# One addition of epsilon and one reciprocal for two blocks of attention probabilities

## The chip, the cores and the metric

The kernel runs on one core of a Trainium2 chip. The time is device microseconds (us) of one execution, and the number compared is the median of the runs.

## What is computed

Three stages follow each other: block-causal attention (4 batches, 8 heads, 576 positions, 64 per head, blocks of 64), a squared-ReLU feed-forward layer on 2304 tokens, and a top-1 mixture of 8 experts. The change touches the first stage alone. Cut to it, the reference is:

```python
scores = q @ k.T / sqrt(64)
scores = where(block_i >= block_j, scores, -1e9)
scores = scores - max(scores)
attn = exp(scores)
attn = attn / (sum(attn) + 1e-9)
out = attn @ v
```

## The kernel before, in words

Attention works on *units*: two heads of one batch, 16 units in all. A unit has nine *blocks* of 64 query rows; with both heads a block fills 128 partitions, and block i sees (i + 1) * 64 keys. So there are 144 steps, one block each, and the loop at L230 runs the parts of several blocks in each step, by three lags (`LAGS = (1, 5, 7)`, L279):

- `scores` (L129) of the block of this step: on GpSimd a memset of 64 columns where i is even (L135); on TensorE three fp32r matmuls (L146), or one fp32 matmul for blocks 0 and 1 (L143); on VectorE the negated row maximum from PSUM (L148); on ScalarE the exponential with the maximum as bias, which also writes the row sum into the small tile `sm` (L153). Block 8 is done in two halves of 288 columns, whose maxima are joined at L151 and whose two sums stand in the two columns of `sm`.
- `normalise` (L157) of the block of one step ago: on VectorE `sm + 1e-9` into `rc` (L164; for block 8, with two sums, L162) and its reciprocal (L165); on GpSimd the product of the block's probabilities `p` with `rc` (L166), 64 to 576 columns wide.
- `p_transpose` (L168) of the block of five steps ago: transpositions of the scaled probabilities on TensorE (L185) and copies from PSUM to SBUF on ScalarE (L191). Blocks 0 and 1, and 2 and 3, are transposed together, when the second of them is due; blocks 4 to 8 each in a step of its own.
- `pv` (L195) seven steps behind blocks 3 and 8: the products with V on TensorE (L208).

In between come, for the next unit, the transpositions of Q and K (L93) and their split in a high and a low part (ScalarE L102 to L126, VectorE L86 and L88, called at the end of the step by `flush`). Weights of the feed-forward layer are converted beside the attention (`convert`, one chunk every four steps from step 8 to step 80, L582): three integer operations on VectorE (L336 to L338), one cast on ScalarE (L371) and one subtraction on GpSimd (L342). From step 50 on, pieces of the feed-forward layer (L385, L460) are run beside the attention.

The tiles of `p` have six buffers, the scores four PSUM banks in the first 36 steps and three after, the transpositions three banks, then two. No order is written out by hand in this stage: the framework's planner fills each engine's queue, starting from the order of the program, the dependencies, the free buffers and its own estimates of durations. On the chip each queue is then worked off strictly in that order.

Of the kernel before, what the change touches and what calls it, by code (L numbers as in the profile page):

```python
# [9 lines left out]
F32 = mybir.dt.float32  # L10
# [4 lines left out]
ALU = mybir.AluOpType  # L15
AX = mybir.AxisListType
PSUM = bass.MemoryType.PSUM
P = 128


def attention(nc, tc, ctx, ps, ident, q, k, v, xT_d):
# [7 lines left out]
    B, H, S, D = q.shape  # L29
# [9 lines left out]
    small = pool("a_small", 8)  # L39
# [16 lines left out]
    st = {}  # L56
# [25 lines left out]
    def flush():  # L82
        while todo:
            scale, o, src, high = todo.pop(0)
            if scale:
                nc.vector.scalar_tensor_tensor(o, src, 0.125, high.bitcast(F32), ALU.mult, ALU.subtract)  # L86
            else:
                nc.vector.tensor_sub(o, src, high.bitcast(F32))  # L88
# [19 lines left out]
    def q_transpose(u):  # L108
        q_high(u, transpose4(st[u]["raw"][0]), slice(0, 8))

    def k_transpose(u):
        kh = kt.tile([P, S], F32R, name="kh", tag="kh")
        kl = kt.tile([P, S], F32R, name="kl", tag="kl")
        kf = kt.tile([P, P], F32, name="kf", tag="kf")
        st[u]["k"] = (kh, kl, kf)
        t = transpose4(st[u]["raw"][1])
        nc.scalar.copy(kf, t[:, 0:P])
        nc.scalar.copy(kh[:, 0:512], t)
        low(False, kl[:, 0:512], t, kh[:, 0:512])

    def tails(u):
        t = ps.t.tile([P, 512], F32, name="te", tag="t")
        nc.tensor.transpose(t[:, 0:P], st[u]["tail"].rearrange("p h d -> p (h d)"), ident)
        q_high(u, t[:, 0:D], slice(8, 9))
        kh, kl, _ = st[u]["k"]
        nc.scalar.copy(kh[:, 512:], t[:, D:2 * D])  # L126
        low(False, kl[:, 512:], t[:, D:2 * D], kh[:, 512:])

    def scores(u, i):  # L129
        kh, kl, kf = st[u]["k"]  # L130
        qh, ql = qb[u % 2]
        n = (i + 1) * D
        pr = pp.tile([P, 640], F32, name="p", tag="p")
        if i % 2 == 0:
            nc.gpsimd.memset(pr[:, n:n + D], 0.0)  # L135
        parts = [(0, n)] if i < 8 else [(0, 288), (288, 288)]
        nm = small.tile([P, 2], F32, name="nm", tag="nm")
        sm = small.tile([P, 2], F32, name="sm", tag="sm")
        scs = []
        for e, (k0, w) in enumerate(parts):  # L140
            sc = ps.s.tile([P, 512], F32, name="sc", tag="s")
            if i < 2:
                nc.tensor.matmul(sc[:, 0:w], qf[u % 2][:, i].rearrange("p h d -> p (h d)"), kf[:, 0:w],  # L143
                                 start=True, stop=True)
            for j, (a, kk) in enumerate(((qh, kh), (qh, kl), (ql, kh)) if i >= 2 else ()):
                nc.tensor.matmul(sc[:, 0:max(w, 256)], a[:, i - 2].rearrange("p h d -> p (h d)"),  # L146
                                 kk[:, k0:k0 + max(w, 256)], start=(j == 0), stop=(j == 2))
            ps.last["max"] = nc.vector.tensor_reduce(nm[:, e:e + 1], sc[:, 0:w], AX.X, ALU.max, negate=True)  # L148
            scs.append(sc)
        if len(parts) == 2:  # L150
            nc.vector.tensor_tensor(nm[:, 0:1], nm[:, 0:1], nm[:, 1:2], ALU.min)  # L151
        for e, (k0, w) in enumerate(parts):
            ps.last["exp"] = nc.scalar.activation(pr[:, k0:k0 + w], scs[e][:, 0:w], AF.Exp, bias=nm[:, 0:1],  # L153
                                                  accum_out=sm[:, e:e + 1])
        st[u][i] = (pr, sm, len(parts))

    def normalise(u, i):  # L157
        n = (i + 1) * D
        pr, sm, k_ = st[u][i]
        rc = small.tile([P, 1], F32, name="rc", tag="rc")  # L160
        if k_ == 2:
            nc.vector.tensor_scalar(rc, sm[:, 0:1], sm[:, 1:2], 1e-9, ALU.add, ALU.add)  # L162
        else:
            nc.vector.tensor_scalar_add(rc, sm[:, 0:1], 1e-9)  # L164
        nc.vector.reciprocal(rc, rc)  # L165
        ps.last["scale"] = nc.gpsimd.tensor_mul(pr[:, 0:n], pr[:, 0:n], rc.to_broadcast([P, n]))  # L166

    def p_transpose(u, blocks):  # L168
        i0 = blocks[0]
        grp = int(i0 >= 4)  # L170
        if i0 == 4 * grp:
            st[u]["pt", grp] = pt.tile(([P, 4, 2, P], [P, 5, 5, P])[grp], F32, name=f"pt{grp}", tag=f"pt{grp}")
        out = st[u]["pt", grp]
        nch = i0 // 2 + 1
        jobs = []
        if grp == 0:
            jobs.append(([(i, c) for i in blocks for c in range(nch)], out[:, i0:i0 + 2, 0:nch]))
        else:
            for c0, c1 in ((0, min(4, nch)), (4, nch)):
                if c1 > c0:  # L180
                    jobs.append(([(i0, c) for c in range(c0, c1)], out[:, i0 - 4, c0:c1]))
        for lst, o in jobs:
            t = ps.t.tile([P, 512], F32, name="tp", tag="t")
            for e, (i, c) in enumerate(lst):
                nc.tensor.transpose(t[:, e * P:(e + 1) * P], st[u][i][0][:, c * P:(c + 1) * P], ident)  # L185
            src = t[:, 0:len(lst) * P]
            if grp == 0:
                src = src.rearrange("p (i c n) -> p i c n", i=2, n=P)
            else:
                src = src.rearrange("p (c n) -> p c n", n=P)  # L190
            P_COPY(nc, i0)(o, src)  # L191
        for i in blocks:
            st[u].pop(i)
# [32 lines left out]
    def at(t):  # L226
        return seq[t] if 0 <= t < len(seq) else (None, None)

    done = 0
    for t in range(len(seq) + LP + 1):  # L230
        u, i = at(t - LT)
        if i in (1, 3):
            p_transpose(u, [i - 1, i])
        elif u is not None and i >= 4:
            p_transpose(u, [i])
        u, i = at(t)
        if u is not None:
            scores(u, i)
            if u + 1 < NU:
                with tc.issue_after(ps.last["exp"].ins) if u == 0 else nullcontext():  # L240
                    if i == 4:
                        q_transpose(u + 1)
                    if i == 5:
                        k_transpose(u + 1)
                if i == 6:
                    tails(u + 1)
            if i == 1 and u == 0:
                load(1, QK)
            if i == (8 if u else 3):
                load(u + 1, V)  # L250
            if i == 7:
                load(u + 2, QK)
        u, i = at(t - LN)
        if u is not None:
            normalise(u, i)
        flush()
        u, i = at(t - LP)
        if i == 3:
            pv(u, 0)
        if i == 8:  # L260
            pv(u, 1)
            done += 1
        yield done
# [1124 lines left out]
```

## Time and profile before

| | |
|---|---|
| median of 3 runs | 909.71 us (908.70 to 909.87) |
| profiled execution, its time | 910.21 us |
| its span, first to last instruction | 908.5 us |
| TensorE busy (share of the span) | 879.4 us (97%) |
| VectorE busy | 640.2 us (70%) |
| ScalarE busy | 569.8 us (63%) |
| GpSimd busy | 217.7 us (24%) |
| granted TensorE clock, mean | 0.996 |

All durations below are from the profiled execution. PE is TensorE's matmul side and PEld its loading of weights, DVE is VectorE, ACT ScalarE, POOL GpSimd. A row of the timeline reads: start, duration (of the whole row, where it merges several instructions), engine, line, operation, output <- input, shape, count; in brackets the idle time of the engine ahead of it and what ended it. Matmuls overlap, so a TensorE that is busy all the time can still have some room.

### The profile page before, as it was taken

What the parts mean: (1) busy time and instruction counts of PE and PEld (TensorE: products, weight loads), DVE (VectorE), ACT (ScalarE), POOL (GpSimd) and SP (SyncE); (2) the same over time, 40 slices, a digit from 0 to 9 for tenths busy, and PEclk for the clock granted to TensorE, in tenths of its full rate; (3) what the DMA queues carried; (4) which work ended last, traced back from release to release, by engine and by line L of the source; (5) the groups of instructions that cost most, each with busy time, mean ns of one, the idle gap of its engine ahead of it and who ended that gap; (6) DMA issues with size and microseconds to landing.
All of it is one profiled execution on the core that took longest, in us unless ns stands there. A gap on an engine that the chain in (4) does not pass through costs nothing. (4 is left out here: it accounts for less than half of the span.)

```text
span 908.5 us, 17049 instructions
## 1 busy us (share of the span) xinstructions
PE 879.4 (97%) x5765; PEld 726.4 (80%) x5765; DVE 640.2 (70%) x1490; ACT 569.8 (63%) x1165; POOL 217.7 (24%) x335
## 2 busy tenths in 40 slices
PE   6889999999999999999999999999999999999996
PEld 5666777888878789999999999998477776776775
DVE  5889986464645446878967777766688888676783
ACT  6888785575757544333566665542287777776773
POOL 4676674142333200000000000002024322222110
PEclk9999999999999999999999999999999999999998
DMA  5766543322220133445112222115345696636601
GB/s 146 174 177 185 143 115 78 100 53 76 77 73 28 54 113 101 155 140 178 56 47 67 74 62 60 44 47 194 109 163 215 229 380 251 223 131 247 197 13 39
DMA packets 109481, 113.84 MB, mean 125 GB/s; under 512 B 62679, under 2 KB 80617, under 8 KB 109387
## 3 DMA queue, kind: packets, MB, share of 16 engines
q1 hardware_dynamic: 105579, 100.74, 35.6%
q0 software_dynamic: 3808, 11.94, 3.7%
q8 instruction: 48, 0.79, 0.4%
q14 instruction: 46, 0.38, 0.2%
HBM read 143.58 MB, written 19.80 MB: 180 GB/s over the span
## 5 line engine op out<-in xcount | busy, mean ns | idle before, releaser
L385 PE MATMUL ph<-xh,wih 128*128 128x256 f32 x576 | 165.8, 288 | 0.0
L385 PE MATMUL ph<-xh,wil 128*128 128x256 f32 x576 | 162.2, 282 | 0.0
L385 PE MATMUL ph<-xl,wih 128*128 128x256 f32 x576 | 162.0, 281 | 0.0
L166 POOL TENSOR_TENSOR p<-p,rc 128x64 f32<-128x64 f32 (+2 forms) x144 | 111.6, 784 | 119.5 <-DVE rc L165 56.7
L385 PEld LDWEIGHTS ph<-xh,wih 128*128 128x128 f32 x576 | 109.0, 189 | 5.3 <-issue 3.1
L385 PEld LDWEIGHTS ph<-xl,wih 128*128 128x128 f32 x576 | 109.2, 190 | 1.1
L385 PEld LDWEIGHTS ph<-xh,wil 128*128 128x128 f32 x576 | 109.2, 190 | 0.4 <-issue 0.4
L148 DVE TENSOR_REDUCE nm<-sc 128x1 f32<-128x288 f32 (+8 forms) x160 | 70.3, 449 | 54.1 <-PE sc L146 45.9
L153 ACT ACTIVATE p<-sc,nm 128x288 f32<-128x288 f32 (+8 forms) x160 | 80.6, 507 | 18.6 <-DVE nm L148 8.1
L1012 DVE TENSOR_TENSOR w1l<-raw,w1h 128x1024 fp32r<-128x1024 f32 x60 | 71.7, 1222 | 23.0 <-ACT w1h L1011 20.5
L1012 DVE TENSOR_TENSOR w2l<-raw,w2h 128x1024 fp32r<-128x1024 f32 x64 | 75.4, 1219 | 10.8 <-ACT w2h L1011 10.7
L1020 POOL DMA_INDIRECT xr<-x_d,gidx_e x2 | 2.3, 1130 | 310.4 <-PE ph L385 310.1
L185 PE MATMUL tp<-ident,p 128*128 128x128 f32 x400 | 65.3, 278 | 6.8 <-POOL p L166 4.5
L395 ACT ACTIVATE r<-ph 128x512 f32<-128x512 f32 x44 | 26.3, 597 | 72.0 <-PE ph L385 71.8
L1011 ACT CAST w2h<-raw 128x1024 fp32r<-128x1024 f32 x64 | 66.1, 1050 | 7.7 <-PE py L1115 7.5
L1011 ACT CAST w1h<-raw 128x1024 fp32r<-128x1024 f32 x60 | 61.6, 1050 | 9.4 <-PE ph L1098 8.7
L191 ACT COPY pt<-tp 128x512 f32<-128x512 f32 (+3 forms) x128 | 61.7, 499 | 8.7 <-PE tp L185 8.2
L185 PEld LDWEIGHTS tp<-ident,p 128*128 128x128 f32 x400 | 46.1, 142 | 18.7 <-POOL p L166 9.5
L396 DVE SCALAR_TENSOR_TENSOR r<-r,sc 128x512 f32<-128x512 f32 x44 | 34.7, 788 | 36.5 <-ACT r L395 36.2
L208 PE MATMUL o<-pt,raw_v 128*64 128x320 f32 (+4 forms) x448 | 55.9, 366 | 1.1 <-ACT pt L191 1.1
L1115 PE MATMUL py<-w2h,hh 128*128 128x512 f32 x128 | 52.1, 407 | 0.0
L1115 PE MATMUL py<-w2h,hl 128*128 128x512 f32 x128 | 50.8, 397 | 0.0
(306 smaller groups left out, 2269.2 us busy)
## 6 DMA issues: line engine op xcount, KB each, us to landing
raw<-in_moe_w_dram SPq DMA_DIRECT2D x172, 512.0 KB
xr<-xT_d SPq DMA_DIRECT2D x19, 512.0 KB
wr<-in_moe_w_in_dram SPq DMA_DIRECT2D x16, 512.0 KB
wr<-in_moe_w_out_dram SPq DMA_DIRECT2D x16, 512.0 KB
row<-part_d SPq DMA_DIRECT2D x20, 256.0 KB
x_d<-row SPq DMA_DIRECT2D x18, 256.5 KB
xT_d<-x SPq DMA_DIRECT2D x16, 288.0 KB
raw_q<-in_q_dram SPq DMA_DIRECT2D x32, 128.0 KB
```

Of the source, the lines that this page charges most:

```text
L148: ps.last["max"] = nc.vector.tensor_reduce(nm[:, e:e + 1], sc[:, 0:w], AX.X, ALU.max, negate=True)
L153: ps.last["exp"] = nc.scalar.activation(pr[:, k0:k0 + w], scs[e][:, 0:w], AF.Exp, bias=nm[:, 0:1], accum_out=sm[:, e:e + 1])
L166: ps.last["scale"] = nc.gpsimd.tensor_mul(pr[:, 0:n], pr[:, 0:n], rc.to_broadcast([P, n]))
L185: nc.tensor.transpose(t[:, e * P:(e + 1) * P], st[u][i][0][:, c * P:(c + 1) * P], ident)
L191: P_COPY(nc, i0)(o, src)
L208: nc.tensor.matmul(o[r, first * D:n], vt[:, c, hh], p[:, first:, c, r], start=(c == 0), stop=(c == cs[-1]))
L385: nc.tensor.matmul(ph[:, e], self.wi[p][w][:, c, e * P:(e + 1) * P], x[a][:, c], start=(n == 0), stop=(n == 3 * KC - 1))
L395: nc.scalar.activation(r, ph.rearrange("p e (t n) -> p (e t) n", n=P), AF.Relu)
L396: nc.vector.scalar_tensor_tensor(r, r, self.sc[:, 0:1], r, ALU.mult, ALU.mult)
L1011: self.nc.scalar.copy(ws[0][c], r)
L1012: self.nc.vector.tensor_sub(ws[1][c], r, ws[0][c].bitcast(F32))
L1115: nc.tensor.matmul(py, hT[a][:, c], self.w2s[w][c // 2][:, c % 2 * D:c % 2 * D + D], start=(t == 0), stop=(t == 3 * KF - 1))
```

## The change

`normalise` is no longer called for every block but for the pairs (0, 1), (2, 3), (4, 5), (6, 7), at the step at which the odd block was normalised before, and for block 8 alone. The two blocks of a pair share one `sm` tile of two columns. One addition and one reciprocal over two columns (128x2 in place of 128x1) give both factors, and GpSimd then does the two multiplications, even block first. The exponentials and the multiplications stay what they were.

```diff
         nm = small.tile([P, 2], F32, name="nm", tag="nm")
-        sm = small.tile([P, 2], F32, name="sm", tag="sm")
+        if i % 2 == 0:
+            st[u]["sm"] = small.tile([P, 2], F32, name="sm", tag="sm")
+        sm = st[u]["sm"]
...
-                                                  accum_out=sm[:, e:e + 1])
-        st[u][i] = (pr, sm, len(parts))
-
-    def normalise(u, i):
-        n = (i + 1) * D
-        pr, sm, k_ = st[u][i]
-        rc = small.tile([P, 1], F32, name="rc", tag="rc")
-        if k_ == 2:
-            nc.vector.tensor_scalar(rc, sm[:, 0:1], sm[:, 1:2], 1e-9, ALU.add, ALU.add)
+                                                  accum_out=sm[:, e + i % 2:e + i % 2 + 1])
+        st[u][i] = (pr, sm)
+
+    def normalise(u, blocks):
+
+        sm = st[u][blocks[0]][1]
+        rc = small.tile([P, 2], F32, name="rc", tag="rc")
+        if len(blocks) == 1:
+            nc.vector.tensor_scalar(rc[:, 0:1], sm[:, 0:1], sm[:, 1:2], 1e-9, ALU.add, ALU.add)
+            nc.vector.reciprocal(rc[:, 0:1], rc[:, 0:1])
         else:
-            nc.vector.tensor_scalar_add(rc, sm[:, 0:1], 1e-9)
-        nc.vector.reciprocal(rc, rc)
-        ps.last["scale"] = nc.gpsimd.tensor_mul(pr[:, 0:n], pr[:, 0:n], rc.to_broadcast([P, n]))
+            nc.vector.tensor_scalar_add(rc, sm, 1e-9)
+            nc.vector.reciprocal(rc, rc)
+        for e, i in enumerate(blocks):
+            n, pr = (i + 1) * D, st[u][i][0]
+            ps.last["scale"] = nc.gpsimd.tensor_mul(pr[:, 0:n], pr[:, 0:n], rc[:, e:e + 1].to_broadcast([P, n]))
...
-        if u is not None:
-            normalise(u, i)
+        if u is not None and (i % 2 or i == 8):
+            normalise(u, [i] if i == 8 else [i - 1, i])
```

## Rows read from the trace of the kernel before

**Rows 1.** Busy time of each engine by stretch; columns as in the first line.

```profile
core 0: us, PE busy (x) PEld busy (x) DVE busy (x) ACT busy (x) POOL busy (x), PEclk, DMA share, GB/s
12.60:82.00 69.40, 59.44 (x422) 45.38 (x421) 60.47 (x203) 61.09 (x201) 47.34 (x81) 1.00 0.65 173
82.00:134.40 52.40, 50.47 (x359) 40.62 (x360) 46.36 (x136) 44.12 (x135) 34.62 (x52) 1.00 0.53 146
134.40:320.00 185.60, 184.25 (x1270) 153.74 (x1269) 97.89 (x308) 117.92 (x340) 65.04 (x131) 1.00 0.24 67
```

**Rows 2.** Groups by line, 12.6 to 82.0 us: busy us, mean ns | idle before.

```profile
L185 PE MATMUL tp<-ident,p 128*128 128x128 f32 x121 | 20.4, 281 | 5.7 <-POOL p L166 4.5 <-ACT pt L191 0.7 <-POOL wil L342 0.3
...
L165 DVE RECIPROCAL rc<-rc 128x1 f32<-128x1 f32 x45 | 6.5, 153 | 0.3
```

**Rows 3.** Lines L164, L151, L336, 12.6 to 82.0 us: ns min/median/max.

```profile
L164 DVE TENSOR_SCALAR rc<-sm x40: 126/142/155, 13.9 to 81.0; 128x1 f32<-128x1 f32 x40
...
L151 DVE TENSOR_TENSOR nm<-nm x5: 146/524/728, 19.8 to 77.4; 128x1 f32<-128x1 f32 x5
...
L336 DVE TENSOR_SCALAR f<-wr x10: 401/712/1262, 23.2 to 81.0; 128x512 int32<-128x512 int32 x10
```

**Rows 4.** Line L779 (the router's addition of epsilon), whole run: ns min/median/max.

```profile
L779 DVE TENSOR_SCALAR sm<-sm x9: 161/167/170, 473.0 to 642.3; 128x2 f32<-128x2 f32 x9
```

**Rows 5.** Timeline around the end of unit 1 (start us, us).

```profile
33.60 0.66 PE L185 MATMUL tp<-ident,p 128*128 128x128 f32 x4
...
34.30 0.59 ACT L191 COPY pt<-tp 128x512 f32<-128x512 f32 x1
34.78 0.51 ACT L153 ACTIVATE p<-sc,nm 128x288 f32<-128x288 f32 x1
34.90 1.04 POOL L166 TENSOR_TENSOR p<-p,rc 128x512 f32<-128x512 f32 x1 [2.68 <-ACT pt L191]
...
37.63 0.33 PE L146 MATMUL sc<-kh,ql 128*128 128x384 f32 x1
38.80 0.77 PE L185 MATMUL tp<-ident,p 128*128 128x128 f32 x5 [0.84 <-POOL p L166]
```

**Rows 6.** Timeline around the end of unit 2.

```profile
47.50 0.94 POOL L166 TENSOR_TENSOR p<-p,rc 128x448 f32<-128x448 f32 x1
...
48.49 0.33 PE L185 MATMUL tp<-ident,p 128*128 128x128 f32 x1 [0.86 <-POOL p L166]
...
48.86 1.04 POOL L166 TENSOR_TENSOR p<-p,rc 128x512 f32<-128x512 f32 x1 [0.42 <-PE tp L185]
...
53.20 0.77 PE L185 MATMUL tp<-ident,p 128*128 128x128 f32 x5 [1.27 <-POOL p L166]
```

**Rows 7.** Timeline around the end of unit 4.

```profile
77.50 0.66 PE L185 MATMUL tp<-ident,p 128*128 128x128 f32 x4
77.78 1.34 POOL L166 TENSOR_TENSOR p<-p,rc 128x512 f32<-128x512 f32 x1 [0.57 <-DVE rc L165]
...
81.99 0.66 PE L185 MATMUL tp<-ident,p 128*128 128x128 f32 x4 [0.68 <-POOL p L166]
```

**Rows 8.** Timeline around the end of unit 0.

```profile
15.90 0.72 POOL L166 TENSOR_TENSOR p<-p,rc 128x320 f32<-128x320 f32 x1
...
18.33 0.50 PE L185 MATMUL tp<-ident,p 128*128 128x128 f32 x3
...
18.80 1.72 POOL L166 TENSOR_TENSOR p<-p,rc 128x384 f32<-128x384 f32 x2 [0.33 <-DVE rc L165]
...
23.79 0.44 PE L185 MATMUL tp<-ident,p 128*128 128x128 f32 x2 [0.49 <-POOL p L166]
```

**Rows 9.** Timeline around the end of unit 3.

```profile
60.41 0.83 POOL L166 TENSOR_TENSOR p<-p,rc 128x384 f32<-128x384 f32 x1 [0.65 <-DVE rc L164]
60.51 0.49 PE L185 MATMUL tp<-ident,p 128*128 128x128 f32 x3
...
62.53 1.08 POOL L166 TENSOR_TENSOR p<-p,rc 128x512 f32<-128x512 f32 x1 [0.23 <-DVE rc L165]
...
64.16 0.60 PE L185 MATMUL tp<-ident,p 128*128 128x128 f32 x4
```

## The prediction

> **What bounds the kernel now.** I read the busy time by stretch first [rows 1], since the page's averages mix stages, and cut it at unit boundaries. From 134.4 us to the end of the attention TensorE is busy for 184.25 of 185.60 us, because pieces of the feed-forward layer fill it; what VectorE or GpSimd do there has cover. The change can only tell ahead of that. From 12.6 to 82.0 us (units 0 to 4, before these pieces) no engine is full: TensorE is busy 59.44 us of 69.40, VectorE 60.47, ScalarE 61.09, GpSimd 47.34. That is a ring of waits between four nearly equally loaded engines, with 9.96 us of TensorE idle; from 82.0 to 134.4 us (units 5 to 7) it is 1.93 us. Then I read what ends TensorE's idle time in the first stretch: 4.5 us of the 5.7 us ahead of the transpositions end with GpSimd's scaling [rows 2]. So the scaled probabilities already come too late for TensorE there, five steps after the scores. Last I read the timeline at the end of each of these five units, where the light blocks 0 to 2 of the next unit make the five steps short [rows 5 to 9]. A reader should look for two starts: that of a scaling on GpSimd and that of the transposition that needs it.
>
> **What goes.** Each of the 64 pairs loses one addition and one reciprocal. In the first stretch that is 20 pairs at 0.142 [rows 3] plus 0.153 us [rows 2], 5.9 us of VectorE. The two that remain have two elements. The nearest row for these is the router's addition of epsilon, the same operation and shape: 0.167 us [rows 4], against 0.142 for one element, so 0.025 more; the reciprocal has no such row, and I give it nothing. That leaves 5.9 - 20 x 0.025 = 5.4 us. How much of it is on the path is bounded by 0 and 5.4. I take a third, 1.8 us: three engines are loaded alike here, and a microsecond of VectorE counts only where its queue is what the others wait for. In units 5 to 7 I take 0 (TensorE's whole idle time of 1.93 us is the bound), and after them 0, covered by the matmuls.
>
> **What is moved.** The scaling of the even block now waits for the odd block's exponential. On the queue of GpSimd the memset of a next `p` tile (L135) and the subtraction of a weight chunk (L342) stand behind this wait; both already stood behind the odd block's own. On VectorE the merged addition waits for what the odd block's addition waited for. No DMA is issued in the moved step, and SyncE's queue isn't passed. For blocks 0 to 3 the wait costs nothing, since a pair is transposed together. Blocks 4 and 6 are transposed alone, one step ahead of their partner. For them I read each unit with one rule: the new scaling of the even block begins where the old one of the odd block began.
>
> - Unit 1: the scaling of block 7 began at 34.90; block 6 takes 0.94 us [rows 6], so it ends at 35.84 where its transposition began at 33.60 [rows 5]: 2.2 us late.
> - Unit 2: 48.86 + 0.94 = 49.80 against 48.49 [rows 6]: 1.3 us.
> - Unit 4: 77.78 + 0.94 = 78.72 against 77.50 [rows 7]: 1.2 us.
> - Unit 0: here it is block 4. Its 0.72 us begin at 18.80 instead of 15.90, and end at 19.52 against a transposition at 18.33: 1.2 us [rows 8]. Block 6 then finds TensorE late already, and I don't count it again.
> - Unit 3: block 4 ends at 60.41 + 0.72 = 61.13 against 60.51, 0.6 us; block 6 would end at 63.47, ahead of 64.16 [rows 9], and costs nothing.
>
> The sum is 6.5 us. Block 7 follows 0.94 us later than now behind block 6, less than block 6's own lateness in units 1, 2 and 4, so it isn't counted a second time. Part of the 6.5 us is absorbed: TensorE waits today for block 8's scaling at the end of the units, 0.49 us in unit 0 [rows 8], 1.27 in unit 2 [rows 6], 0.68 in unit 4 [rows 7], together 2.4 us, and a TensorE that comes late waits that much less. In unit 1 the 0.84 us [rows 5] don't help: on ScalarE the copy of block 6 (34.30) stands directly ahead of block 8's exponential (34.78), so a late copy makes block 8 late as well. What is left is 4.1 us; the bounds are 0 (the planner finds other matmuls for each gap) and 6.5 us.
>
> **The sum.** -1.8 + 4.1 = +2.3 us. The profiled execution took 910.21 us (span 908.5 and 1.7 around it) and would take 912.5. The median of the runs stands 0.5 us below it, so I forecast 909.7 + 2.3 = 912.0 us. About 0.2%, 1.8 us, is what a measurement of this kernel can tell from no change, so this is just past it.
>
> **The rivals.**
>
> *VectorE's relief wins (faster).* Place: the queue of VectorE in units 0 to 4. Price: with the lateness wholly covered, the gain is 1.8 to 5.4 us, 3.6 in the middle, which gives 906.1 us. It decides from the point on where the planner, which now sees the even block ready a step later, puts scores of coming blocks ahead of the transposition. For it: in unit 1 it did this already, the scores of block 5 end just before the transposition of block 8 starts (37.63 and 38.80 [rows 5]). Against it: score banks are few, and each such score must be reduced and exponentiated before the next can follow.
>
> *Both cancel (no change).* If half of the 6.5 us is covered and the relief is between a third and two thirds of 5.4 us, the difference is within 1.8 us; 909.7 us. TensorE's full queue after 134.4 us speaks for it only in that nothing is added later.
>
> *The two-element addition is held while GpSimd works (slower still).* VectorE's small operations differ in this trace: the addition on one element never took over 0.155 us, though GpSimd was busy two thirds of that stretch. But L151, also one element, with two inputs from SBUF, took 0.146 to 0.728, and L336, one input and two constants like our addition but 512 elements wide, 0.401 to 1.262, with a median 0.31 us over its minimum [rows 3]. Those two are held, by whatever GpSimd is running, for up to 0.86 us. If the addition on two elements joins them, 20 x 0.31 = 6.2 us are added against the 5.4 saved: 0.8 us more work, a third of it 0.3 us. Everything behind it in VectorE's queue, the maxima above all, then comes later too, block 8 included, and nothing of the 6.5 us is absorbed: 909.7 + 6.5 + 0.3 = 916.5 us. It decides from a hold of 0.27 us per pair (5.4 / 20), where the relief is gone. Against it stands the router's addition on two elements, steady at 0.161 to 0.170 [rows 4], which however ran between 473 and 642 us, long after the attention and its scalings.
>
> [...]
>
> **How the numbers follow.** The late even blocks at 912.0 us get 0.32, the held addition at 916.5 us 0.10, the relief at 906.1 us 0.30, the cancelling 0.28. Slower by over 0.2% is 0.32 + 0.10 = 0.42, within 0.2% 0.28, faster 0.30. The forecast alone holds from 909.7 - 0.3 (nothing more absorbed than is gained) to 909.7 + 6.5 - 1.8, so from 909.4 to 914.4 us. The range reaches down to 905.0, near the full relief (904.3), and up to 917.0, just over the held addition; about a tenth is left out on each side.
>
> **What would show it.** Right: additions and reciprocals at 64 and 80 where they were 128 and 144; more idle time ahead of L185 ended by L166 than 4.5 us in the first five units; these units together longer than 69.4 us; nothing changed after 134.4 us but the start. Wrong: the first five units shorter than 69.4 us with TensorE's wait for the scaling no longer than now (relief); a median of the new additions at 0.3 us and over (held); or a difference that arises after 134.4 us, from a new order of the queues, of which this sum knows nothing.

## The result, and the profile after

The changed kernel takes 919.65 us (median of 6 runs, 915.85 to 923.45) against 910.08 us of the kernel before (median of 6 as well, 908.70 to 911.48), a ratio of 1.0109 with the interval [1.0094, 1.0123]. The forecast was 912.0 us, the range 905 to 917: the direction was right, the loss forecast was a quarter of the one measured, and the range was missed. The profiled execution is the longest of the runs: 923.45 us, span 921.8, mean granted clock 0.988.

In the code of the changed kernel the scores' matmuls are L148, the maxima L150, the exponential L155, block 8's addition and reciprocal L164 and L165, a pair's L167 and L168, the scaling L171, the transpositions L190 and their copies L196.

First the page of the changed kernel, its busy time: VectorE issues 128 instructions less than before and is busy for as long as before (639.2 us against 640.2).

```profile
PE 886.7 (96%) x5765; PEld 731.6 (79%) x5765; DVE 639.2 (69%) x1362; ACT 571.1 (62%) x1165; POOL 216.5 (23%) x335
```

Then the busy time by stretch, cut at the starts of the same units: 0 to 4, 5 to 7, 8 and 9. Of the changed kernel:

```profile
core 0: us, PE busy (x) PEld busy (x) DVE busy (x) ACT busy (x) POOL busy (x), PEclk, DMA share, GB/s
12.60:85.30 72.70, 62.09 (x407) 46.23 (x405) 60.53 (x156) 58.47 (x190) 43.95 (x77) 0.95 0.60 161
85.30:137.20 51.90, 48.50 (x344) 38.58 (x343) 45.78 (x107) 42.97 (x131) 34.45 (x53) 1.00 0.54 152
137.20:191.60 54.40, 51.66 (x350) 43.51 (x350) 28.77 (x76) 33.06 (x97) 20.15 (x43) 0.97 0.28 74
```

Of the kernel before, by the same units (the cuts of [rows 1] lie elsewhere):

```profile
12.60:79.10 66.50, 57.36 (x408) 43.76 (x407) 57.66 (x194) 58.47 (x191) 44.44 (x78) 1.00 0.63 167
79.10:130.40 51.30, 48.65 (x343) 38.64 (x344) 45.99 (x132) 42.74 (x131) 35.21 (x53) 1.00 0.60 167
130.40:182.60 52.20, 50.97 (x349) 42.46 (x349) 29.14 (x92) 32.63 (x97) 20.28 (x43) 1.00 0.30 78
```

Units 0 to 4 are 6.2 us longer, units 5 to 7 0.6 us, units 8 and 9 2.2 us. In units 0 to 4 TensorE's idle time grew only from 9.14 to 10.61 us; the larger part, 4.7 us, shows as busy time with as many matmuls. Two things stretch a busy TensorE: the clock (0.95 there: two stretches of 3.4 us, from 19.9 and 54.0 us, with 0.50 and 0.51 of the clock granted, by estimate worth at most half of their 6.8 us, 3.4 of the 4.7), and broken streams: one transposition alone shows 0.33 us [rows 6], four in a row 0.66 us together [rows 5]. The idle column alone would hide most of the loss.

The wait that the prediction turned on is that of the transpositions for GpSimd's scaling. In units 0 to 4 it hardly grew, from 3.5 us to 3.9 us. The group of the kernel before (12.6 to 79.1 us), then that of the changed kernel (12.6 to 85.3 us):

```profile
L185 PE MATMUL tp<-ident,p 128*128 128x128 f32 x116 | 19.3, 280 | 4.6 <-POOL p L166 3.5 <-ACT pt L191 0.7 <-POOL wil L342 0.3
...
L190 PE MATMUL tp<-ident,p 128*128 128x128 f32 x116 | 21.0, 300 | 5.5 <-POOL p L171 3.9 <-DVE ql L86 1.0 <-ACT pt L196 0.4
```

Last the groups of VectorE in units 0 to 4 of the changed kernel (busy us, mean ns | idle before):

```profile
L167 DVE TENSOR_SCALAR rc<-sm 128x2 f32<-128x2 f32 x19 | 7.3, 387 | 1.2 <-ACT p L155 1.1
L168 DVE RECIPROCAL rc<-rc 128x2 f32<-128x2 f32 x20 | 3.2, 158 | 0.2
```

The same two lines over the whole attention (ns min/median/max):

```profile
L167 DVE TENSOR_SCALAR rc<-sm x64: 141/161/1071, 12.0 to 326.5; 128x2 f32<-128x2 f32 x64
...
L168 DVE RECIPROCAL rc<-rc x64: 145/164/168, 13.7 to 326.7; 128x2 f32<-128x2 f32 x64
```

The reciprocal did what was hoped: half as many, at 158 ns instead of 153 [rows 2]. The addition didn't. Its median is 161 ns, but in units 0 to 4 its mean is 387 ns, where one column never took over 155 [rows 3]. One instance in the changed kernel's timeline shows why:

```profile
38.80 1.15 POOL L171 TENSOR_TENSOR p<-p,rc 128x576 f32<-128x576 f32 x1
...
38.90 1.07 DVE L167 TENSOR_SCALAR rc<-sm 128x2 f32<-128x2 f32 x1
...
39.88 0.41 DVE L341 TENSOR_SCALAR f<-wr 128x512 int32<-128x512 int32 x1
```

The addition starts 0.1 us into a scaling on GpSimd and ends 0.02 us after it. Seven of the 20 additions of units 0 to 4 are held so and take 0.38 to 1.07 us.

The late even block is there too. Unit 1 in the changed kernel, to be read against [rows 5]: counted from the unit's first exponential (21.6 us before, 22.9 now), block 6's transposition starts 14.9 us in and not 12.0.

```profile
36.52 0.16 DVE L168 RECIPROCAL rc<-rc 128x2 f32<-128x2 f32 x1
...
36.82 1.93 POOL L171 TENSOR_TENSOR p<-p,rc 128x448 f32<-128x448 f32 x2 [2.91 <-DVE rc L168]
...
37.81 0.66 PE L190 MATMUL tp<-ident,p 128*128 128x128 f32 x4 [0.17 <-POOL p L171]
```

What nothing in the prediction had is at 156 us, in unit 9. There the tables of the router are made: GpSimd's iotas (L664), their casts on VectorE (L666). In the changed kernel:

```profile
153.09 0.19 DVE L666 CAST down<-down_i 128x8 f32<-128x8 int32 x1 [1.24 <-POOL down_i L664]
...
153.21 1.15 POOL L171 TENSOR_TENSOR p<-p,rc 128x576 f32<-128x576 f32 x1
...
153.28 1.16 DVE L666 CAST col<-col_i 128x128 f32<-128x128 int32 x1
...
155.68 0.73 DVE L403 SCALAR_TENSOR_TENSOR gl<-r,sc,gh 128x512 fp32r<-128x512 f32 x1
...
156.47 0.79 PE L465 MATMUL pxa<-woh,gl 128*128 128x512 f32 x1 [2.34 <-DVE gl L403]
```

The same place in the kernel before:

```profile
148.22 0.73 DVE L398 SCALAR_TENSOR_TENSOR gl<-r,sc,gh 128x512 fp32r<-128x512 f32 x1
...
149.01 0.50 PE L460 MATMUL pxa<-woh,gl 128*128 128x512 f32 x1 [1.02 <-DVE rc L164]
```

A cast waits for GpSimd, the next takes 1.16 us beside a scaling of 1.15, and `gl`, which TensorE's next product needs, stands behind all casts in VectorE's queue: its last input was written by 152.41 us, VectorE was idle until 153.09, and `gl` starts at 155.68. TensorE waits 2.34 us where it waited 1.02. After that its clock falls. Stretches of the changed kernel, same columns as above:

```profile
50.00:54.00 4.00, 2.66 (x18) 1.68 (x19) 3.20 (x7) 4.00 (x14) 2.99 (x6) 1.00 0.74 194
54.00:57.40 3.40, 3.40 (x15) 3.01 (x15) 3.05 (x10) 1.70 (x6) 2.10 (x2) 0.51 0.34 112
150.00:156.40 6.40, 4.13 (x36) 3.71 (x33) 4.84 (x15) 3.52 (x12) 5.62 (x15) 1.00 0.38 94
156.40:159.90 3.50, 3.43 (x14) 3.24 (x15) 1.89 (x6) 0.72 (x1) 1.01 (x2) 0.51 0.00 0
```

TensorE is busy for 2.66 of 4.00 us, then 0.51 of the clock is granted for 3.4 us; the same after 4.13 of 6.40 us. By estimate from the 0.51, such a stretch costs up to half of its 3.4 us. This execution has three in the attention (from 19.9, 54.0 and 156.4 us) and two later (351.0 and 699.2), the one of before a single one (685.5), the last microseconds of both aside.

### The profile page after: what moved, and what is told of

Same layout as the page of the kernel before. It is cut to its first block, busy times and chain, and to the rows that moved or that the text cites. A ratio compares the mean times of both kernels' runs of the same rounds, so it can differ in the third digit from the quotient of the medians.

```text
span 921.8 us, 16849 instructions
## 1 busy us (share of the span) xinstructions
PE 886.7 (96%) x5765; PEld 731.6 (79%) x5765; DVE 639.2 (69%) x1362; ACT 571.1 (62%) x1165; POOL 216.5 (23%) x335
## 5 line engine op out<-in xcount | busy, mean ns | idle before, releaser
L171 POOL TENSOR_TENSOR p<-p,rc 128x64 f32<-128x64 f32 (+2 forms) x144 | 109.3, 780 | 88.5 <-DVE rc L168 66.2
L150 DVE TENSOR_REDUCE nm<-sc 128x1 f32<-128x288 f32 (+8 forms) x160 | 70.4, 451 | 61.8 <-PE sc L148 54.3
L155 ACT ACTIVATE p<-sc,nm 128x288 f32<-128x288 f32 (+8 forms) x160 | 80.5, 507 | 20.3 <-DVE nm L150 9.6
L1017 DVE TENSOR_TENSOR w1l<-raw,w1h 128x1024 fp32r<-128x1024 f32 x60 | 71.7, 1223 | 22.9 <-ACT w1h L1016 19.8
L190 PE MATMUL tp<-ident,p 128*128 128x128 f32 x400 | 67.4, 284 | 9.1 <-POOL p L171 6.2
L196 ACT COPY pt<-tp 128x512 f32<-128x512 f32 (+3 forms) x128 | 61.8, 497 | 12.8 <-PE tp L190 12.3
L190 PEld LDWEIGHTS tp<-ident,p 128*128 128x128 f32 x400 | 47.1, 145 | 22.8 <-POOL p L171 11.8
L148 PE MATMUL sc<-kh,qh 128*128 128x256 f32 (+5 forms) x128 | 49.3, 386 | 2.5 <-ACT p L155 2.4
```

Of the source, the lines that this page charges most:

```text
L1017: self.nc.vector.tensor_sub(ws[1][c], r, ws[0][c].bitcast(F32))
```

## The experiments

The next table has for every kernel the median and, from its profile, how much later than in the kernel before units 5, 8 and 10 and the attention's last exponential start (before: 79.1, 130.4, 182.6, 317.7 us). Two profiles of kernels with the same or nearly the same order differ by up to 1.5 us in these columns (late_only and late_grouped, where one profile has a fall of the clock that the other lacks). Ratios are against the kernel before in the same set of runs (its medians 909.28 to 910.08 us).

| kernel | us | ratio | unit 5 | unit 8 | unit 10 | end |
|---|---|---|---|---|---|---|
| changed kernel | 919.65 | 1.0109 | +6.2 | +6.8 | +9.0 | +9.6 |
| after_again | 920.10 | 1.0113 [1.0097, 1.0128] | +6.8 | +7.3 | +9.6 | +10.2 |
| hold_only | 910.63 | 1.0017 [1.0006, 1.0028] | +0.5 | +0.7 | +1.1 | +1.0 |
| late_only | 912.98 | 1.0033 [1.0020, 1.0046] | +0.1 | +2.1 | +4.1 | +4.0 |
| late_grouped | 912.78 | 1.0028 [1.0018, 1.0038] | +0.3 | +2.3 | +2.7 | +2.5 |
| split_add | 916.49 | 1.0080 [1.0066, 1.0094] | +2.5 | +6.0 | +6.7 | +7.0 |
| late_extra_recip | 917.13 | 1.0084 [1.0070, 1.0098] | +2.5 | +5.1 | +5.7 | +6.1 |
| pairs_no_add | 912.79 | 1.0045 [1.0028, 1.0062] | +2.2 | +2.8 | +3.9 | +3.9 |
| before_no_add | 907.38 | 0.9980 [0.9970, 0.9991] | -0.2 | +0.6 | +0.1 | -0.1 |
| pairs_0_to_3 | 910.67 | 1.0011 [1.0002, 1.0019] | +1.5 | +1.7 | +1.7 | +1.9 |
| pairs_4_to_7 | 915.68 | 1.0064 [1.0048, 1.0080] | +3.0 | +3.9 | +6.0 | +6.5 |
| pairs_0_to_3_no_add | 907.36 | 0.9977 [0.9968, 0.9986] | -1.0 | -1.7 | -2.4 | -2.4 |
| pairs_lag6 | 920.21 | 1.0119 [1.0103, 1.0134] | +2.0 | +4.6 | +7.3 | +9.0 |
| before_router_late | 908.08 | 0.9984 [0.9975, 0.9993] | -0.6 | -0.7 | -1.9 | -1.9 |
| hold_router_late | 909.10 | 0.9990 [0.9981, 0.9999] | +1.6 | +1.8 | +0.6 | +0.6 |
| late_router_late | 909.99 | 1.0002 [0.9993, 1.0011] | +0.8 | +2.8 | +1.0 | +0.9 |
| split_router_late | 914.84 | 1.0061 [1.0047, 1.0075] | +2.9 | +5.3 | +3.4 | +4.1 |
| after_router_late | 914.17 | 1.0052 [1.0032, 1.0072] | +6.8 | +7.4 | +5.5 | +6.6 |
| pairs_0_to_3_no_add_router_late | 905.29 | 0.9958 [0.9944, 0.9971] | -1.0 | -1.7 | -3.6 | -3.6 |

One more measure is needed to read these runs: how late each kernel's even blocks really are. The next table has, for blocks 4 and 6 of all 16 units, the mean time from the end of the block's own exponential to the start of its scaling, and how many of these 32 scalings start before the odd partner's exponential has ended. It is taken from the traces.

| kernel | us after the own exponential | ahead of the partner's exponential |
|---|---|---|
| before | 1.78 | 20 of 32 |
| late_only, late_grouped | 2.45 | 15 of 32 |
| pairs_no_add | 3.78 | 0 of 32 |
| split_add | 4.26 | 0 of 32 |
| late_extra_recip | 4.29 | 0 of 32 |
| changed kernel | 4.43 | 0 of 32 |

**hold_only.** Every block keeps its own step; only the odd block's addition runs over two columns. Against the changed kernel:

```diff
+        i = blocks[0]
+        e = i % 2
+        if e:
+            nc.vector.tensor_scalar_add(rc, sm, 1e-9)
...
-        if u is not None and (i % 2 or i == 8):
-            normalise(u, [i] if i == 8 else [i - 1, i])
+        if u is not None:
+            normalise(u, [i])
```

> Every block is normalised in its own step as before, with its own addition and reciprocal; only the odd block's addition runs over two columns (128x2), of which one result is not used. So 64 additions can be held by GpSimd, nothing is late, nothing is saved. Theory hold (the two-element addition is held and stalls VectorE's queue): median of these 64 additions well over 0.2 us in the first five units, time 913 to 916 us. Theory late (the even blocks scaled a step later make the loss): the additions may be held, but the time is 910 to 911.5 us.

910.63 us, as theory late had it. TensorE, ScalarE and GpSimd work in the order of the kernel before. The two widths stand side by side in this kernel's trace:

```profile
L166 DVE TENSOR_SCALAR rc<-sm x64: 142/169/1081, 12.4 to 317.9; 128x2 f32<-128x2 f32 x64
...
L168 DVE TENSOR_SCALAR rc<-sm x64: 126/144/155, 11.8 to 314.5; 128x1 f32<-128x1 f32 x64
```

So the hold goes with the second column. In the order of before it costs 1 to 1.5 us, although an addition takes up to 1.08 us and more additions are held than in the changed kernel (23 of 64 take over 0.2 us here, 12 there).

**late_only.** Both normalisations of a pair are called at the odd block's step, with the old instructions on one column:

```diff
-            nc.vector.tensor_scalar_add(rc, sm, 1e-9)
-            nc.vector.reciprocal(rc, rc)
+            for e in range(2):
+                nc.vector.tensor_scalar_add(rc[:, e:e + 1], sm[:, e:e + 1], 1e-9)
+                nc.vector.reciprocal(rc[:, e:e + 1], rc[:, e:e + 1])
```

> The pairs are normalised at the odd block's step, GpSimd scales them one after the other, as in the changed kernel; but each block keeps its own one-element addition and reciprocal, so there is no hold and no relief. Theory late: 915 to 919 us, at least two thirds of the loss of 9.6 us. Theory hold: 910 to 912 us.

912.98 us, 3.5 us over before, between the two expectations. Nothing of it arises ahead of unit 5 and 2 us by unit 8; another 2 us come between units 8 and 10, with a wait of 2.15 us ahead of the product with `gl` at 151.5 us and a clock at 0.50 from 152.8 us.

But this kernel isn't the test of lateness that it was meant to be. With its own addition and reciprocal the even block no longer depends on the odd one, and in the planner's queues 15 of the 32 even blocks are scaled ahead of their partner's exponential. In unit 1 block 6 is the second scaling of the first row; block 7's exponential only follows:

```profile
30.50 1.72 POOL L172 TENSOR_TENSOR p<-p,rc 128x384 f32<-128x384 f32 x2 [0.32 <-ACT x L216]
31.72 0.69 ACT L155 ACTIVATE p<-sc,nm 128x512 f32<-128x512 f32 x1
```

The same two in split_add (below), where the shared reciprocal makes block 6 wait:

```profile
32.32 0.69 ACT L155 ACTIVATE p<-sc,nm 128x512 f32<-128x512 f32 x1
...
35.44 1.93 POOL L172 TENSOR_TENSOR p<-p,rc 128x448 f32<-128x448 f32 x2 [2.90 <-DVE rc L169]
```

late_only has about a quarter of the change's lateness (2.45 us against 1.78 before and 4.43 in the changed kernel), so its 3.5 us are not the price of the late blocks.

**pairs_no_add.** The changed kernel without the addition for blocks 0 to 7:

```diff
-            nc.vector.tensor_scalar_add(rc, sm, 1e-9)
-            nc.vector.reciprocal(rc, rc)
+            nc.vector.reciprocal(rc, sm)
```

> The changed kernel without the addition of 1e-9 for the paired blocks (left out; block 8 keeps it): the reciprocal is taken from the sums, two at a time. The held addition is gone and VectorE has 64 instructions less than the changed kernel, the lateness stays. Theory late: 914 to 918 us. Theory hold: 908 to 911 us, since the relief of VectorE is then real.

912.79 us, between the two expectations. Without the addition 7 of the 10 us are gone, more than the hold costs in hold_only. All pairs are late here and nothing is held; against the kernel before without the addition (before_no_add, next) this is 5.4 us more.

**before_no_add.** The same in the kernel before (`rc_` is the tile that `rc` was):

```diff
-            nc.vector.tensor_scalar_add(rc, sm[:, 0:1], 1e-9)
-        nc.vector.reciprocal(rc, rc)
+            rc = sm[:, 0:1]
+        nc.vector.reciprocal(rc_, rc)
...
```

> The kernel before without the addition of 1e-9 for blocks 0 to 7 (left out; block 8 keeps it): 128 instructions less on VectorE, 40 of them in the first five units, 5.7 us, with nothing late and nothing held. If VectorE's relief is worth a third, 907 to 909 us; if it is on the path, 904 to 906 us; if it is worth nothing there, 909.5 to 911 us. The planner's new order can shift each of these by some us.

907.38 us, inside the 907 to 909 us of a worth of a third. 128 additions of 0.14 us, 18 us by their durations, are worth 1.9 us; in the profile VectorE's busy time falls by 10.7 us (640.2 to 629.5). The planner's new order is part of these 1.9 us.

**after_again.** The changed kernel once more, beside the following three.

> The changed kernel once more, to have it beside the experiments on one chip and with a second trace. If part of its loss is TensorE's clock falling to its lower level at times, runs with a mean granted clock of 0.996 and over are at 915 to 917 us, runs below 0.990 at 921 us and over, and the median is between 917 and 921. If the clock is only a companion of the loss, the times of runs with high and low clock agree within 1.5 us.

920.10 us (916.97 to 920.46). The clocks of these five runs lie between 0.990 and 0.995, so neither of the two clock limits written down was reached; the run at 0.995 is the one of 916.97 us, the four at 0.990 to 0.992 took 919.56 to 920.46. They lie some 3 us apart, more than the 1.5 us of a clock that is only a companion.

**split_add.** Late pairs, one reciprocal over two columns, but two additions on one column each:

```diff
-            nc.vector.tensor_scalar_add(rc, sm, 1e-9)
+            for e in range(2):
+                nc.vector.tensor_scalar_add(rc[:, e:e + 1], sm[:, e:e + 1], 1e-9)
             nc.vector.reciprocal(rc, rc)
```

> The changed kernel with the shared addition split into two additions of one element each, which nothing holds; the reciprocal stays shared, GpSimd still scales in pairs. Theory late and held together (a held addition costs most where the scaling behind it is late already): 911.5 to 914 us, as with late_only. Theory order (the planner's new order makes the loss, held or not): 916 us and over.

916.49 us. No addition is held here (128 of them, longest 0.157 us), the even blocks are nearly as late as in the changed kernel (4.26 us), and 7 us of the loss remain: late pairs cost that much without any hold. This was written down as the sign of a loss by the new order; since late_only was hardly late, it is no less one of a loss by lateness. The medians leave 3.2 us to the held addition; TensorE's order is nearly that of the changed kernel (24 of its 2055 matmuls in the attention's time stand elsewhere). Units 0 to 4, to be held against 66.50 us before:

```profile
12.60:81.60 69.00, 59.42 (x405) 44.54 (x405) 57.25 (x176) 57.77 (x190) 43.60 (x77) 1.00 0.64 168
```

At full clock 2.1 us of the 2.5 us more show as busy time of TensorE, as in the changed kernel.

**pairs_lag6.** The changed kernel with transpositions and products one step later:

```diff
-LAGS = (1, 5, 7)
-NPBUF = 6
+LAGS = (1, 6, 8)
+NPBUF = 7
```

> The changed kernel with the transpositions six steps behind the scores in place of five, the products with V eight in place of seven, and seven buffers of p in place of six. Theory late: the late scaling has its step back, the wait of TensorE for it ahead of 80 us goes, 908 to 912 us. Theory hold (VectorE's queue is what costs): 915 us and over. The longer way alone may cost or give a microsecond; its control would be the kernel before with the same lags.

920.21 us. The wait that the prediction turned on falls to 2.1 us (4.5 in the kernel before, 5.3 in the changed kernel), and another takes its place, that for the copies out of PSUM. TensorE's waits in this kernel from 12.6 to 140 us (total us, times, longest):

```profile
PE tw L93 <- ACT pt L196: 3.0, 5, 1.0
PE tp L190 <- ACT pt L196: 2.5, 6, 0.9
PE tp L190 <- POOL p L171: 2.1, 3, 1.4
```

Slack for the late block alone doesn't repair the change. What the longer lags cost by themselves is not known: the kernel before with them wasn't tried.

**pairs_0_to_3_no_add.** Only the pairs that are transposed together share a reciprocal, and blocks 0 to 7 have no addition:

```diff
-        if u is not None and (i % 2 or i == 8):
-            normalise(u, [i] if i == 8 else [i - 1, i])
+        if u is not None and i >= 4:
+            normalise(u, [i])
+        elif i in (1, 3):
+            normalise(u, [i - 1, i])
...
```

> Only blocks 0 and 1, and 2 and 3, which are transposed together anyway, are normalised in pairs with one reciprocal; blocks 4 to 8 each in its own step. The addition of 1e-9 is left out but for block 8. So nothing is late, nothing is held, and VectorE has 160 instructions less than the kernel before. If relief without lateness and hold is a gain: 905 to 908 us, at or below the kernel before without the addition. If the pair's joint scaling costs by itself: 909 us and over.

907.36 us, as before_no_add: the shared reciprocal of these pairs adds nothing that can be measured.

**pairs_0_to_3 and pairs_4_to_7.** The same split with the addition kept, and the other half:

```diff
-        if u is not None and (i % 2 or i == 8):
-            normalise(u, [i] if i == 8 else [i - 1, i])
+        if u is not None and (i < 4 or i == 8):
+            normalise(u, [i])
+        elif i in (5, 7):
+            normalise(u, [i - 1, i])
...
```

> Only the pairs (0, 1) and (2, 3), which are transposed together in any case, share an addition and a reciprocal; blocks 4 to 7 are normalised one by one as before. The additions on two columns stay (32 of them), no block is scaled later than its transposition needs it. Theory (the held addition costs little by itself, the loss needs blocks 4 and 6 to be late): 909 to 911.5 us, unit 5 starts at most 1 us later than before. Rival (the held addition in the new order of the queues is enough): 913 us or more, unit 5 starts at least 2 us later.

> The other half: only the pairs (4, 5) and (6, 7) share an addition and a reciprocal; blocks 0 to 3 are normalised one by one as before. Theory (the loss needs the late even blocks): 914 to 918 us, most of the 10 us of the full change, unit 5 starts 3 to 5 us later than before. Rival (the loss goes with the number of held additions, 32 of 64): about 5 us, 914 us or less, and as much as the kernel with the pairs 0 to 3 alone shows.

910.67 and 915.68 us: with 32 two-column additions each, the pairs whose even block becomes late carry 6 us, the others 1. So most of the loss goes with the pairs in which blocks 4 and 6 have to wait. Unit 5 starts 1.5 us late in the first, more than the 1 us written down and less than the rival's 2. The two halves sum to 7.4 us, not to 10.

**after_router_late and before_router_late.** GpSimd's instructions of the router's setup are queued behind the attention's last scaling; TensorE's order stays:

```diff
-    rt.open(ctx, tc, ps_g, NT - begun * TB)
+    with tc.issue_after(banks.last["scale"].ins):
+        rt.open(ctx, tc, ps_g, NT - begun * TB)
```

> The changed kernel, but GpSimd's part of the router's setup is queued behind the attention's last scaling (before: between the 80th and the 82nd scaling, at about 150 us). TensorE's, ScalarE's and VectorE's orders stay the same but for the copies of these tables. Theory (the 2.4 us that the changed kernel loses between the starts of units 8 and 10 are a collision of the later pair with this setup, and the fall of the clock at 156 us comes from it): the drift between units 8 and 10 goes from +2.3 to +0.5 us or less, no low clock near 156 us, 916 to 918 us. Rival (an ordinary late scaling, the setup only happens to stand there): drift and time as the changed kernel, 919 to 921 us.

> Control: the kernel before with the same move of the router's setup. Theory and rival: within 1 us of the kernel before, 908.5 to 910 us, since TensorE waits only 0.5 to 1.0 us there. If it gains as much as the changed kernel does with this move, the setup has nothing to do with the change.

914.17 us (912.39 to 918.25) and 908.08 us, both below what was expected. The move gives 5.5 us to the changed kernel and 1.4 us to the one before. Units 8 and 9 of the changed kernel with the move, to be held against 54.40 and 52.20 us above:

```profile
137.90:188.10 50.20, 49.79 (x350) 41.99 (x349) 27.37 (x68) 32.74 (x94) 18.86 (x33) 1.00 0.30 81
```

TensorE is full, the clock stays up, and the stretch is 4.2 us shorter than without the move. In the kernel before the move shortens it from 52.20 us to 50.90:

```profile
129.80:180.70 50.90, 50.68 (x349) 42.44 (x348) 27.84 (x84) 32.62 (x95) 18.29 (x33) 1.00 0.30 80
```

So 2.9 us by the profiles, 4.1 by the medians, are a collision of the change with this setup, which in the old order cost TensorE little. By the intervals of the ratios it can be 1 to 6 us.

**late_router_late and split_router_late.** The same move in these two.

> late_only with the same move of the setup. If late_only's 3.7 us are half this collision: 909.5 to 911 us, with no drift of over 0.5 us between units 8 and 10. If they are plain late scaling in units 6 to 9: 911.5 to 913 us.

> split_add with GpSimd's part of the router's setup behind the last scaling. If the setup's collision comes from late scaling alone and is independent of the hold: between the starts of units 8 and 10 the drift falls by 3 us or more, 911.5 to 913.5 us. If it needs the held addition: as much as the kernel before gains by this move, 1.4 us, 914.5 to 916 us.

909.99 and 914.84 us, 3.0 and 1.65 us less than without the move. The first gains twice what the kernel before gains, as half a collision had it, the second about as much, as the theory had it in which the collision needs the held addition. But in its profile split_router_late's units 8 and 9 (135.7 to 185.9) take the same 50.20 us, so the median of split_add shows less of the collision than its trace, and that theory isn't settled.

**late_extra_recip and late_grouped.** In the code only a shared reciprocal lies between late_only and split_add, yet 3.5 us. late_extra_recip is split_add with a third, unused reciprocal; late_grouped is late_only with both additions ahead of both reciprocals.

```diff
             nc.vector.reciprocal(rc, rc)
+            nc.vector.reciprocal(small.tile([P, 1], F32, name="rx", tag="rx"), rc[:, 1:2])
```

```diff
             for e in range(2):
                 nc.vector.tensor_scalar_add(rc[:, e:e + 1], sm[:, e:e + 1], 1e-9)
+            for e in range(2):
                 nc.vector.reciprocal(rc[:, e:e + 1], rc[:, e:e + 1])
```

> As split_add (two additions on one column, one shared reciprocal at the odd block's step), with a third, unused reciprocal on one column behind it, so VectorE has as many instructions as in late_only, while TensorE's order stays near split_add's. If the planner's order makes the difference between late_only (913.0 us) and split_add (916.5): 915.5 to 918 us. If late_only is cheaper for another reason (VectorE's load, the earlier reciprocal of the even block): 912 to 914 us.

> As late_only, but both additions on one column come first and then both reciprocals on one column, so the even block's factor is ready later by an addition, as in split_add. TensorE's order is late_only's but for one matmul. If the planner's order makes the difference between late_only (913.0 us) and split_add (916.5): 912 to 914 us. If it is the even block's later factor: 915.5 us or more.

917.13 and 912.78 us. VectorE's load is excluded as the reason for the difference, and the shared reciprocal itself takes 0.168 us at most. The even block's later factor is not excluded: late_grouped's even blocks are scaled no later than late_only's (2.45 us), and those of split_add and late_extra_recip 1.8 us later. What the second pair of kernels has and the first lacks is thus the full lateness, and with it another order on TensorE, ScalarE and GpSimd; these runs don't separate the two. TensorE's waits from 12.6 to 140 us show no large change. late_only:

```profile
PE tp L191 <- POOL p L172: 7.0, 12, 1.5
PE sc L148 <- ACT p L155: 1.3, 2, 0.8
...
PE sc L145 <- ACT p L155: 0.4, 1, 0.4
```

split_add:

```profile
PE tp L191 <- POOL p L172: 6.0, 13, 1.9
PE sc L148 <- ACT p L155: 2.7, 4, 1.3
...
PE sc L145 <- ACT p L155: 1.5, 3, 0.7
```

The kernel before:

```profile
PE tp L185 <- POOL p L166: 4.5, 6, 1.3
PE sc L146 <- ACT p L153: 1.7, 2, 1.2
PE sc L143 <- ACT p L153: 1.5, 3, 0.8
```

The waits for the scaling are alike in late_only and split_add; those of the scores for the exponentials (for a free bank) go from 1.7 to 4.2 us, but they are 3.2 us in the kernel before, which is the fastest of the three. Neither wait alone tells the price of the late blocks.

**hold_router_late.** hold_only with the setup moved.

> hold_only with GpSimd's part of the router's setup behind the last scaling, in the order of the kernel before, which with this move takes 908.1 us. If the held additions cost their time wherever they stand: 909.3 us or more. If they cost only by way of the setup's collision: 908 to 908.7 us.

909.10 us, between the two expectations and nearer the first: in the old order the held additions cost 0.5 to 1.0 us over before_router_late (by the ratios, whose intervals overlap, and by the medians), with the setup moved as with it in place.

**pairs_0_to_3_no_add_router_late.** What helped, together.

> What helped, put together: one reciprocal for the pairs (0, 1) and (2, 3) only, no addition of epsilon for blocks 0 to 7 (left out as in the two kernels without it; the largest exponential of a row is 1, so in fp32 a sum of at least 1 plus 1e-9 is the sum itself), the router's setup behind the last scaling. If the gains add up: 907.4 - 1.4 = 906.0 us, ratio 0.996. If both take the same idle time of TensorE: 907 to 908 us.

905.29 us, ratio 0.9958 [0.9944, 0.9971]: the gains add up, and this is the fastest of all. Its units 0 to 4 (12.6 to 78.1 us) are 1.0 us shorter than before:

```profile
12.60:78.10 65.50, 57.89 (x412) 44.66 (x411) 54.62 (x145) 57.74 (x190) 46.41 (x77) 1.00 0.67 178
```

## Why the prediction was wrong

The medians with the setup where it was and behind the last scaling:

| | in place | moved |
|---|---|---|
| before | 909.5 | 908.1 |
| + held addition, old order (hold_only) | 910.6 | 909.1 |
| a quarter of the lateness, old additions (late_only) | 913.0 | 910.0 |
| late pairs with a shared reciprocal, old additions (split_add) | 916.5 | 914.8 |
| + held addition (changed kernel) | 919.7 | 914.2 |

Two steps failed: the price of the late even blocks, 4.1 us in the sum and 5 to 7 us in the runs, and that of the new addition, 0.025 us a pair in the sum and 0.245 us in units 0 to 4 of the trace.

- **The late even blocks, +4.1 us.** That late even blocks cost is borne out: the halves of the change put 6 us on the pairs whose even block becomes late. The size was too small. Without a held addition late pairs cost 7 us (split_add), and 5.4 us with no additions on either side (pairs_no_add against before_no_add); the 6.5 us that the prediction added up before it took off 2.4 us for block 8's waits was nearer. The rule "the new scaling begins where the old one of the odd block began" held within 1.1 us by each unit's own clock, but for unit 3 (block 4 begins 2.5 us later). What failed is the step from there to the path. In unit 1 the transposition is 2.9 us late and the next unit starts only 0.4 us later. Over units 0 to 4 TensorE's wait for the scaling grew by 0.4 us in the changed kernel; the loss stands mostly in its busy time.
- **Nothing after 82.0 us, and nothing after 134.4.** In split_add only 2.5 us arise ahead of unit 5, the other 4.5 us after it. For units 5 to 7 the prediction gave a bound for the gain and no price for the lateness. After 134.4 us a TensorE busy for 184.25 of 185.60 us [rows 1] was taken for cover. It is cover only while its own next operand isn't behind the moved work: `gl` is made on VectorE, the queue that the change rearranges, and in unit 9 that queue also waits for GpSimd (1.24 us ahead of the first cast; 2.34 us of TensorE for `gl`). The move of the setup shows 2.9 us (profiles) to 4.1 us (medians) of the 10 us to be this.
- **The held addition, chance 0.10.** The sum priced the new addition at 0.167 us by the router's [rows 4], made long after the scalings; L336 [rows 3], from the stretch in question, was the row to go by. Its mechanism came true: held while GpSimd works, mean 387 ns, a hold of 0.245 us a pair, just short of the 0.27 us from which the relief was to be gone. Its 916.5 us was the nearest of the four cases. The price isn't a constant: about 1 us in the old order, 3.2 us in the changed kernel's median, nothing measurable with the setup moved.
- **The relief, -1.8 us.** The bound of 5.4 us was as good as used up by the hold: 20 additions at 387 - 142 = 245 ns more are 4.9 us. A third as the worth of VectorE's time fits before_no_add, where 5.7 us of additions go in the first five units and 1.9 us are gained; 18 us go in the whole attention and the profile doesn't show where the gain arises, so the fit can be luck. In split_add the reciprocals saved are worth nothing measurable (late_extra_recip, which spends that time again, takes 0.6 us more).
- **The queues' order.** Named only as what would make the sum wrong, and given no price. The planner orders the queues anew when the pairs are late, and no run here has the lateness without the new order, so how much of the 5 to 7 us is order stays open.
- **The clock.** The sum had no term for it. Of the 11 runs of the changed kernel the two at a mean clock of 0.995 or more took 915.85 and 916.97 us, the one at 0.988 took 923.45. The first two are as fast as split_add (916.01 to 918.11 at 0.994 to 0.997), so the 3.2 us of the held addition go with these stretches at about half the clock (0.50 and 0.51 in the profile) and aren't a cost beside them; this was read from the runs and not tried by itself.

The hold itself is in the traces of both kernels. In the kernel before L151 took 146 ns in each of the two instances of the first five units with no scaling of GpSimd beside it, and 524 to 728 ns in the three beside one, ending 0.01 to 0.02 us after it (the one from 47.73 us takes 0.72 us, beside the scaling of 0.94 us from 47.50 us in [rows 6]); L336 took 401 and 418 ns where no scaling ran at its start and 639 to 1262 ns in the other eight. The addition took 141 to 1071 ns at two columns and 126 to 155 at one (hold_only); the instance at 38.90 us ends with GpSimd's scaling. Of the 12 shared additions of the changed kernel that start with 0.15 us or more of a scaling or subtraction on GpSimd still to run, 11 took 0.38 us or more and one (at 55.33 us) 0.155. The reciprocal on the same two columns was never held (145 to 168 ns, five of the 64 started beside such an instruction, 149 to 166); why not, no run here shows.

With the setup moved the hold's 3.2 us are no longer to be seen in the medians. The runs of after_router_late suggest why: at a clock of 0.997 or more three of the six took 912.39 to 913.03 us, as split_router_late does there (912.53 and 913.33), the other three, at 0.992 to 0.994, 915.32 to 918.25, and the median lies between. What stays open is what decides in a run whether the clock falls, and what in the late pairs is dear, the wait itself or TensorE's new order, which wasn't tried piece by piece.

## What to carry to other kernels

Count an instruction saved on an engine only after looking at its wider successor beside what runs at the same time: two columns instead of one took the mean of this addition from 142 to 387 ns. A full engine is no cover where its own operands come out of the queue that the change rearranges (here `gl`, for which TensorE waited 2.34 us, 1.02 before); look along the whole run for other work that joins those queues (here a setup of some 3 us). Where a planner orders the queues, look in the trace whether a variant does what its edit says before reading its time: late_only was to make the even blocks late, and the planner scaled 15 of 32 ahead of their partners all the same.

## What was not expected of the hardware

The reciprocal over two columns was never held in 64 instances (145 to 168 ns), where the addition over the same tile took up to 1.07 us beside a GpSimd instruction. TensorE's granted clock was 0.51 for 3.4 us after 4.00 us with 2.66 us busy, in which no single wait took over 0.45 us, and again after the 6.40 us with the wait of 2.34 us. And 128 instructions or 10.7 us of busy time less on the second busiest engine gave 1.9 us.
